# The FFN's second product, from the second group on, as seven block products in place of eight

## The chip, the cores and the metric

The kernel runs on one core of a Trainium2 chip. The metric is the device time of one execution in microseconds (us); less is better. The profile adds one execution that the hardware profiler recorded, with the time of each instruction on each engine: PE (TensorE, matmuls; PEld, its weight loads), DVE (VectorE), ACT (ScalarE), POOL (GpSimd) and SP (SyncE, which issues most DMAs).

## The reference

Attention with four sink keys and a window of 128, a Fourier mix over positions and features, a LayerNorm and an FFN:

```python
keep = is_sink | in_window                    # 4 sinks, window 128
a = softmax(where(keep, q @ k.T / sqrt(64), -1e9))
x = concat_heads(a @ v)                       # [4, 768, 512]
u = x + real(fft(fft(x, axis=1), axis=2))
un = (u - mean(u)) / sqrt(var(u) + 1e-06)
out = u + relu(un @ w_ch1) @ w_ch2            # 512 -> 2048 -> 512
```

There are 4 x 768 = 3072 rows. The weights arrive as 64-bit floats; everything else is fp32.

## The kernel before

Rows are taken in 24 blocks of 128, six to a batch. The first part of the program (up to about 222 us) computes attention and the Fourier mix and leaves u in SBUF or DRAM; its order is not touched by the change. The FFN follows, in groups of blocks (`sizes`): 4, 2, 4, 4, 4, 4, 2. The 2048 hidden features are 16 chunks f of 128.

Every fp32 operand of a product is split in a high and a low part of the matmul's input type, and a product is three matmuls (high x high, high x low, low x high). For each group and each f:

- `ch1` (L609): 4 x 3 = 12 matmuls of W1's chunk f against un, transposed, over all the group's rows at once (512 columns for four blocks, 256 for two), into one PSUM bank of two that take turns;
- `relu` (L1099, ACT) writes the high part of relu(h) to SBUF and `relu_lo` (L1104, DVE) the low part, from PSUM;
- `ch2` (L1111): for each block three matmuls with 512 columns, that block's h as weights and W2's chunk f moving, summed over f in one bank for each block.

`advance` (L1215) issues the ch2 of the step before behind the ch1 of the present one, so PE alternates between 12 matmuls of each kind. After f = 15, `finish` adds u to each bank on DVE (L1115) and stores the block (L1116, SP). During a group, `prepare` (L1138) makes the next group's un: LayerNorm's statistics (L504, L505), the inverse deviations (a chain of small steps, `deviations`), un itself (`un_make`, L528), its transposition, and the split in high (`un_hi`, L538, ACT) and low (`un_lo`, L543, DVE). In groups 1 and 2 the transposition is on PE (`un_turn`, L534), from group 3 on it is 16 small transposes for a block on DVE (L1135). It is a generator; three of its steps run for each f. Group 0's un is turned on PE too.

Group 0's FFN (222 to 335 us) also converts the weights: `convert` (L574) makes fp32 of the two words of a 64-bit value in three DVE steps (L580 to L582), the high part on ACT (L597) and the low part on POOL (L598), for W1 and W2 alike. Both parts of all the weights then stay in SBUF. Some are kept in tiles that earlier stages had used: `w_ring` (f = 0, 1), and `gh` and `gl` of the Fourier mix (`W_FOLD`). Up to the end of group 0 a scheduler orders the instructions; from group 1 on the loop at L1224 to L1241 is a manual schedule, and each engine runs in the order of the code.

Of the kernel before, what the change touches and what calls it, by code (L numbers as in the profile page):

```python
# [46 lines left out]
W_FOLD = 12  # L47
# [7 lines left out]
PREP_N = 3  # L55
PREP_AT, PREP_M = 1, 3
RELOAD_AT = 1
# [86 lines left out]
PARTS_TAIL = ((1,) * 5, 1, 1)  # L144

# [60 lines left out]
def kernel(  # L206
# [17 lines left out]
    def f32(ap):  # L224
        return ap.bitcast(F32)
# [25 lines left out]
    sizes = [4, 2, 4, 4, 4, 4, 2]  # L251
# [8 lines left out]
    def run(general):  # L260
        tag = "g" if general else ""
        with ExitStack() as p1:
# [301 lines left out]
            Wt, raw, state = {}, {}, {}  # L564
# [8 lines left out]

            def convert(i, pool=None):  # L574

                r = raw.pop(i)
                t = npool.tile([P, 512], I32, tag="qs0", name=f"cv{i}", bufs=QSB)
# [12 lines left out]
                elif W_FOLD <= i < W_FOLD + NHALF:  # L590

                    if i == W_FOLD:
                        state["fold"] = [npool.tile([P, NHALF, DM], F32R, tag=t, name=f"w_{t}", bufs=1) for t in ("gh", "gl")]
                    d = [t[:, i - W_FOLD] for t in state["fold"]]
# [4 lines left out]
                Wt[divmod(i, 2)] = d  # L599
# [13 lines left out]
            def start_ffn(s):  # L613
                state["h"] = p1.enter_context(tc.tile_pool(name="ps_h" + tag, bufs=2, space=PSUM))
# [470 lines left out]
            wa = p1.enter_context(tc.tile_pool(name="wa" + tag, bufs=1, side="right"))  # L1085
            pg = ExitStack()
            g0 = pg.enter_context(tc.tile_pool(name="g0" + tag, bufs=1, side="right"))
            def relu(g, f, ps):
                tb = P * len(groups[g])
                if g == 0 and un_last:  # L1090

                    t = un_last[0][:, 1].rearrange("p i c t -> p (i c t)")
                    h = [t[:, 1024 * (f % 2) + 512 * i:1024 * (f % 2) + 512 * i + 512] for i in range(2)]
                elif g == 0:
                    h = [g0.tile([P, tb], F32R, tag=f"h{i}", name=f"h{i}_{g}_{f}", bufs=2) for i in range(2)]
                else:
                    h = npool.tile([P, 2, tb], F32R, tag="ld", name=f"h_{g}_{f}", bufs=LDB)
                    h = [h[:, 0], h[:, 1]]
# [7 lines left out]
            def ch2(f, h, po):  # L1106
                w = Wt[f, 1]
                for i in range(len(po)):
# [29 lines left out]
            def prepare(g):  # L1138
# [12 lines left out]
                for i, u in enumerate(us):  # L1151
# [3 lines left out]
                    if g <= 2:  # L1155

                        pool, tag = banks[1 if g == 1 else i % 2][:2]
# [9 lines left out]
                    un_hi(b, blk, unT, i)  # L1167
                    un_lo(b, blk, unT, i)
# [4 lines left out]
            un_last = []  # L1173
            with (tc.manual_schedule() if MAN0 else ExitStack()):
# [10 lines left out]
                for f in range(NF):  # L1185
                    ps = hp.pop(0) if f < 2 else ch1(0, f, unT0)
                    if f == PREP:
# [3 lines left out]
                        un_last.append(wl.tile([P, 2, 2, NCC, 2 * P], F32R, name="un_last"))  # L1191
                    hs[f] = relu(0, f, ps)
# [18 lines left out]
                ch2(NF - 1, hs.pop(NF - 1), po)  # L1211
# [121 lines left out]
```

## Time and profile before

| | |
|---|---|
| median of three runs | 789.29 us (788.75 to 790.04) |
| time of the profiled execution | 788.91 us |
| its span, first to last instruction | 787.1 us |
| PE, DVE, ACT, POOL busy | 759.0, 457.9, 238.6, 177.3 us |
| granted TensorE clock, mean | 0.994 |
| group 0's FFN | about 222 to 335 us |
| groups 1 to 6 | 335 to 779 us |

A row of the timeline has start, duration, engine, line and operation, with the written tile on the left of the arrow, the read ones on its right, and then the count. In brackets stands how long the engine had been idle and on what. In the chain of waits, a row has start, duration and what ran. In a group of instructions, count and busy time stand behind the bar or the x, then the mean of one in ns, then the idle time ahead of them and who ended it. In the page's table of 40 slices each digit is a tenth of a slice:

```profile
PE   7999998999989899999999999999999999999996
DVE  6788588888899699662356514662356424511211
ACT  5777665665632223211111110111111111110110
POOL 2566377377635345300000000000000000000000
```

### The profile page before, as it was taken

The numbers are of one execution on the slowest core, as the hardware profiler recorded it, in microseconds if no ns is written. First come the engines' busy times: TensorE is split into PE (matmuls) and PEld (weight loads), VectorE is DVE, ScalarE is ACT, GpSimd is POOL, SyncE is SP. The second block draws the span as 40 slices with busy tenths as digits, with TensorE's granted clock in tenths as the row PEclk, the third lists the DMA queues.
The fourth block names the chain that finished last, engine by engine and source line by source line (L and its number), as shares of the span: only waits on it lengthen the run. The fifth ranks groups of instructions, "written<-read, shape, count | busy, mean of one in ns | idle before, by whom it ended". The sixth has DMA issues, their size and how long they took to land.

```text
span 787.1 us, 11962 instructions
## 1 busy us (share of the span) xinstructions
PE 759.0 (96%) x4379; PEld 614.3 (78%) x4379; DVE 457.9 (58%) x1354; ACT 238.6 (30%) x704; POOL 177.3 (23%) x283
## 2 busy tenths in 40 slices
PE   7999998999989899999999999999999999999996
PEld 5666776766778778899888888888888888888895
DVE  6788588888899699662356514662356424511211
ACT  5777665665632223211111110111111111110110
POOL 2566377377635345300000000000000000000000
PEclk9999999999999999999999999999999999999998
DMA  9844516433214356120100002000200001000100
GB/s 307 268 115 137 139 55 197 127 111 130 68 33 154 135 187 214 55 107 1 54 1 0 1 0 107 1 1 0 81 1 0 1 5 49 1 1 0 54 1 32
DMA packets 41811, 57.68 MB, mean 73 GB/s; under 512 B 2796, under 2 KB 27500, under 8 KB 41360
## 3 DMA queue, kind: packets, MB, share of 16 engines
q1 hardware_dynamic: 41456, 53.07, 21.2%
q0 software_dynamic: 288, 3.76, 1.2%
q8 instruction: 37, 0.61, 0.3%
q14 instruction: 30, 0.25, 0.1%
HBM read 47.37 MB, written 9.45 MB: 72 GB/s over the span
## 4 chain that ended last, share of the span: by engine, by line
PE 82%; DVE 11%; issue 2%; ACT 2%; POOL 1%; DMA 1%; SPq 0%; ACTq 0%; DVEq 0%; POOLq 0%
PE o L1111 32%; PE h L609 32%; PE xt L779 4%; PE s L692 4%; PE pt L741 2%; PE za L384 2%; DVE f L341 1%; PE zb L384 1%; DVE cv L581 1%; DVE cv L580 1%; PE x L791 1%; DVE sm L710 1%; PE zr L384 1%; DVE cv L582 1%; DVE gl L357 1%
## 5 line engine op out<-in xcount | busy, mean ns | idle before, releaser
L1111 PE MATMUL o<-w,h 128*128 128x512 f32 x876 | 216.9, 395 | 0.0
L1104 DVE SCALAR_TENSOR_TENSOR h<-h,h 128x512 fp32r<-128x512 f32 (+1 forms) x107 | 65.4, 611 | 243.8 <-ACT h L1099 243.6
L1111 PEld LDWEIGHTS o<-w,h 128*128 128x128 f32 x876 | 164.0, 189 | 34.5
L1099 ACT ACTIVATE h<-h 128x512 fp32r<-128x512 f32 (+1 forms) x107 | 57.1, 534 | 360.5 <-PE h L609 360.5
L609 PE MATMUL h<-un_slots,w 128*128 128x512 f32 (+1 forms) x576 | 123.7, 363 | 0.9 <-POOL w L598 0.9
L609 PEld LDWEIGHTS h<-un_slots,w 128*128 128x128 f32 x576 | 99.8, 188 | 19.4 <-POOL w L598 1.4
L609 PE MATMUL h<-un_last,w 128*128 128x512 f32 (+1 forms) x432 | 88.6, 354 | 0.0
L609 PEld LDWEIGHTS h<-un_last,w 128*128 128x128 f32 x432 | 72.8, 189 | 12.4
L716 ACT ACTIVATE sm<-sm,mx 128x132 f32<-128x132 f32 x192 | 75.9, 400 | 14.4 <-DVE mx L710 14.4
L1135 DVE STREAM_TRANSPOSE unf<-un 32x128 f32<-32x128 f32 x224 | 67.7, 302 | 3.2
L692 PE MATMUL s<-ring,q 64*128 64x260 f32 x320 | 55.1, 426 | 7.6 <-DVE mx L710 7.5
L710 DVE CUSTOM_DVE_ANT_0 sm<-s,mask 128x132 f32<-128x132 f32 x192 | 47.5, 284 | 3.9 <-PE s L690 2.0
L698 DVE COPY_PREDICATED s<-older,s 128x256 f32<-128x256 uint8 x80 | 33.7, 422 | 14.5 <-PE s L692 14.3
L692 PEld LDWEIGHTS s<-ring,q 64*128 64x128 f32 x320 | 24.8, 185 | 21.7 <-issue 10.3
L598 POOL TENSOR_TENSOR w<-cv,w 128x512 fp32r<-128x512 f32 x25 | 33.7, 1349 | 31.1 <-ACT w L597 31.1
L779 PE MATMUL xt<-ptl,ldv 128*64 128x128 f32 x384 | 39.0, 285 | 0.0
L716 ACT ACTIVATION_READ_ACCUMULATOR sm<-sm,mx 128x1 f32 x192 | 36.8, 192 | 0.0
L1111 PE MATMUL o<-w_ring,h 128*128 128x512 f32 x144 | 35.6, 393 | 0.0
L757 POOL TENSOR_SCALAR_AFFINE_SELECT ptl<-pta 128x512 f32<-128x512 f32 x48 | 32.4, 675 | 13.4 <-ACT pta L748 10.1
L748 ACT COPY pta<-pt 128x512 f32<-128x512 f32 x48 | 28.0, 584 | 19.1 <-PE pt L741 18.5
L779 PEld LDWEIGHTS xt<-ptl,ldv 128*64 128x64 f32 x384 | 21.8, 136 | 14.2 <-issue 6.9
L779 PE MATMUL xt<-pta,ldv 128*64 128x128 f32 x320 | 31.7, 274 | 0.1
(197 smaller groups left out, 1042.3 us busy)
## 6 DMA issues: line engine op xcount, KB each, us to landing
raw<-in_moe_w_ch_dram SPq DMA_DIRECT2D x32, 512.0 KB, 3.5
ldv<-in_v_dram SPq DMA_DIRECT2D x28, 256.0 KB, 2.7
ring<-in_qk_dram SPq DMA_DIRECT2D x24, 264.0 KB, 4.7
out_dram<-u SPq DMA_DIRECT2D x24, 256.0 KB, 3.6
q<-in_qk_dram SPq DMA_DIRECT2D x20, 256.0 KB, 4.8
cst<-in_dft_dram POOLq DMA_DIRECT2D x1, 3348.0 KB, 12.9
ud<-us SPq DMA_DIRECT2D x12, 256.0 KB, 2.1
u<-ud SPq DMA_DIRECT2D x2, 1024.0 KB, 4.9
```

The costliest lines, as they stand in the source:

```text
L598: G.tensor_tensor(d[1], tf, f32(d[0]), op=ALU.subtract)
L609: T.matmul(ps[:, :tb], a[:, cs], x[:, :, cc, :], start=n == 0, stop=n == 3 * NCC - 1)
L692: T.matmul(ps[:, j, :P + W], st["q", g][rows, hp, :], keys(g, 2 * hp + j), start=True, stop=True)
L698: V.copy_predicated(ps[:, :, P + NS:P + W], older[qi > 2], ps[:, :, 0:P])
L710: V.tensor_tensor_reduce(sm[:, h % 4], ps[:, j, P:P + W], mask[min(qi, 3)], -SCALE, 3.0e38, ALU.add, ALU.min, accum_out=mx[:, 0, h:h + 1])
L716: A.activation(sm[:, h % 4], sm[:, h % 4], AF.Exp, bias=mx[:, 0, h:h + 1], scale=-1.0, accum_out=mx[:, 1, h:h + 1])
L757: G.affine_select(lo, a, [[0, 4], [s, P]], compare_op=ALU.is_ge, fill=0.0, base=0, channel_multiplier=-s)
L779: T.matmul(ps[D * j:D * j + D, p, :], st["v", kb(g) - i][:, h, :], a[:, h % 4, :], start=i == 0, stop=i == n - 1)
L1099: A.activation(h[0], ps[:, :tb], AF.Relu)
L1104: V.scalar_tensor_tensor(h[1], ps[:, :tb], 0.0, f32(h[0]), op0=ALU.max, op1=ALU.subtract)
L1111: T.matmul(po[i], a[:, ts_], x, start=f == 0 and n == 0, stop=f == NF - 1 and n == 2)
L1135: V.transpose(unf[32 * q:32 * q + 32, :, r], un[r].rearrange("p (c q j) -> p c q j", c=NCC, q=4)[:, :, q])
```

## The change

All groups have four blocks. Group 0's second product stays as it was. From group 1 on the second product of two chunks f (2q and 2q + 1) is taken as a product of 2 x 2 blocks. The left matrix is h: two row halves (the group's first and last two blocks, A1x and A2x) by two chunks. The right one is W2: two chunks by two halves of 256 output columns. Seven products of sums of such blocks replace the eight (Strassen's scheme in Winograd's form). With S1 = A21 + A22, S2 = S1 - A11, S3 = A11 - A21, S4 = A12 - S2 and the sums T1 to T4 on W2's side, the left factors are, in order, A11, S3, A12, A22, S1, S2, S4. The seven products are summed over q in seven PSUM banks, so ch1 has one bank (`h0`) from then on. A product is two row tiles x 3 matmuls of 256 columns, 42 for a pair of chunks in place of 24 of 512.

The sums are made in fp32 and split afterwards. So relu writes fp32 (`r4`), and DVE makes S1 to S4 (L1252 to L1261), ACT the high parts (L1247) and DVE the low parts (L1248). W2 stays in fp32 (`w2r`); for each group and pair, POOL makes T1 to T4 (L1272 to L1275), ACT copies their high parts (L1283) and POOL subtracts for the low parts (L1284); in the last group DVE takes two of these. Group 0 keeps W2's split parts in three turning tiles, and POOL rebuilds W2 for f = 0 and 1 from them. The tiles of split sums are single. PE issues, for each q, ch1 of 2q, the first half of the products of q - 1 (`slot`, products 0, 1, 2 and half of 3), ch1 of 2q + 1, and the second half. At a group's end the seven sums are combined and added to u: `finish_a` (a copy on ACT and four additions on DVE), `finish_b` (one) and `finish_c` (four) run in the first two pairs of the next group, `finish_d` (three additions on POOL, then the stores) in the pairs after. `finish_last` does it for the last group. `prepare` of group 1 has four blocks, turned on PE; from group 2 on all is turned on DVE.

```diff
-W_FOLD = 12
+W_FOLD = 6
...
-PREP_N = 3
+PREP_N = 4
...
-RELOAD_AT = 1
+RELOAD_AT = 4
...
+LEFT = ("A11", "S3", "A12", "A22", "S1", "S2", "S4")
+RIGHT = (0, 0), (1, 0), (0, 1), (1, 1), (2, 0), (2, 1), (3, 0)
...
-    sizes = [4, 2, 4, 4, 4, 4, 2]
+    sizes = [4] * 6
...
+                if which and f >= 2:
+                    t = w2_raw(f, pool)
...
+                    d = state["w2t", f % 3]
...
-                ps = state["h"].tile([P, 512], F32, tag="h", name=f"h_{g}_{f}")
+                ps = state["h"].tile([P, 512], F32, tag=f"h{f % 2 if g == 0 else 0}", name=f"h_{g}_{f}")
...
+            for f in range(2):
+                G.tensor_tensor(w2_raw(f, wa).bitcast(F32), *(f32(x) for x in Wt[f, 1]), op=ALU.add)
...
-                    if g <= 2:
-
-                        pool, tag = banks[1 if g == 1 else i % 2][:2]
+                    if g == 1:
+                        pool, tag = banks[1][:2]
...
+                    if g > 1:
+                        yield
...
+                        hc.append(wl.tile([P, 2, len(LEFT) * 2 * P], F32R, name="h_sums"))
+                        hc.append(wl.tile([P, 2, 2 * P], F32R, name="w2t3"))
...
-                ch2(NF - 1, hs.pop(NF - 1), po)
-                finish(0, po, us)
...
+            sums = [npool.tile([P, 4, 2 * P], F32, tag="ld", name=f"sums{i}", bufs=LDB) for i in range(3)]
+            r4, hs4, wt4 = sums
+            r4 = r4.rearrange("p (f t) w -> p f t w", f=2)
+            hc_hi, hc_lo = hc[0][:, 0], hc[0][:, 1]
+            WC = [state["w2t", i] for i in (1, 2, 0)] + [[hc[1][:, i] for i in range(2)]]
...
+            def split_h(src, a, n):
+                A.copy(hc_hi[:, left(a, n)], src)
+                V.tensor_tensor(hc_lo[:, left(a, n)], src, f32(hc_hi[:, left(a, n)]), op=ALU.subtract)
+            def first_h():
+                V.tensor_tensor(hs4[:, 0], r4[:, 0, 0], r4[:, 0, 1], op=ALU.subtract)
+                split_h(r4[:, 0, 0], 0, 1)
+                split_h(hs4[:, 0], 1, 1)
+            def second_h():
+                V.tensor_tensor(hs4[:, 1], r4[:, 0, 1], r4[:, 1, 1], op=ALU.add)
+                split_h(r4[:, 1].rearrange("p t w -> p (t w)"), 2, 2)
+                V.tensor_tensor(hs4[:, 2], hs4[:, 1], r4[:, 0, 0], op=ALU.subtract)
+                V.tensor_tensor(hs4[:, 3], r4[:, 1, 0], hs4[:, 2], op=ALU.subtract)
+            def third_h():
+                split_h(hs4[:, 1:4].rearrange("p t w -> p (t w)"), 4, 3)
+            def w_sums(q):
+                x = Wr[q].bitcast(F32).rearrange("p f (d w) -> p f d w", d=2)
+                (b11, b12), (b21, b22) = [[x[:, i, j] for j in range(2)] for i in range(2)]
+                t3, t4, t1, t2 = (wt4[:, i] for i in range(4))
+                G.tensor_tensor(t3, b22, b12, op=ALU.subtract)
+                G.tensor_tensor(t1, b12, b11, op=ALU.subtract)
+                G.tensor_tensor(t2, b22, t1, op=ALU.subtract)
+                G.tensor_tensor(t4, b21, t2, op=ALU.subtract)
+            def split_w(q, i, eng=G):
+                x = Wr[q].bitcast(F32).rearrange("p f (d w) -> p f d w", d=2)
+                c, k, src, n = ((0, 0, x[:, :, 0], 2), (1, 0, wt4[:, 0:1], 1), (1, 1, wt4[:, 1:2], 1),
+                                (2, 0, wt4[:, 2:4], 2), (3, 0, x[:, 1:2, 1], 1))[i]
+                hi, lo = (t[:, 2 * P * k:2 * P * (k + n)].rearrange("p (n w) -> p n w", n=n) for t in WC[c])
+                A.copy(hi, src)
+                eng.tensor_tensor(lo, src, f32(hi), op=ALU.subtract)
+            def product(acc, q, i, tp):
+                a, (c, k) = i, RIGHT[i]
+                hi, lo = (t[:, 2 * P * a + P * tp:2 * P * a + P * tp + P] for t in (hc_hi, hc_lo))
+                w_hi, w_lo = (t[:, 2 * P * k:2 * P * k + 2 * P] for t in WC[c])
+                for n, (x, w) in enumerate(((hi, w_hi), (hi, w_lo), (lo, w_hi))):
+                    T.matmul(acc[i][:, 2 * P * tp:2 * P * tp + 2 * P], x, w, start=q == 0 and tp == 0 and n == 0,
+                             stop=q == NF // 2 - 1 and n == 2, skip_group_check=True)
...
+            def finish_a(g, acc):
+                (x11, _), (x21, x22) = halves(g)
+                p1, p7, p2 = (bank2(acc[i]) for i in range(3))
+                state["u2"] = s = wl.tile([P, 2, 2 * P], F32, tag="u2", name=f"u2_{g}", bufs=1)
+                A.copy(s, p1)
+                add(V, x11, p1)
+                add(V, x21, p7)
+                add(V, x22, p7)
+                add(V, x11, p2)
+            def finish_b(g, acc):
+                add(V, halves(g)[1][0], bank2(acc[3]))
+            def finish_c(g, acc):
+                (x11, x12), (x21, x22) = halves(g)
+                p5, p6, p3 = (bank2(acc[i]) for i in range(4, 7))
+                s = state["u2"]
+                add(V, x12, p5)
+                add(V, x22, p5)
+                add(V, s, p6)
+                add(V, x12, p3)
+            def finish_d(g):
+                (_, x12), (x21, x22) = halves(g)
+                for x in (x12, x21, x22):
+                    add(G, x, state["u2"])
+                    yield
+                for t in (0, 1):
+                    for b, blk in groups[g][2 * t:2 * t + 2]:
+                        nc.sync.dma_start(out[b, blk], u_of(b, blk))
+            def slot(item, part):
+                if item is None:
+                    return
+                g, acc, q = item
+                for i, tp in [(i, tp) for i in range(7) for tp in range(2)][part]:
+                    product(acc, q, i, tp)
+            def finish_last(g, acc, q):
+                (x11, x12), (x21, x22) = halves(g)
+                p1, p7, p2, p4, p5, p6, p3 = (bank2(t) for t in acc)
+                s1, s2 = wl.tile([P, 2, 2 * P], F32, tag="u2", name=f"u2_{g}", bufs=1), r4[:, 0]
+                for i in range(4):
+                    for tp in range(2):
+                        product(acc, q, i, tp)
+                A.copy(s1, p1)
+                add(G, x11, s1)
+                add(V, x21, p4)
+                add(V, x11, p2)
+                for i in (5, 4, 6):
+                    for tp in range(2):
+                        product(acc, q, i, tp)
+                add(V, s1, p6)
+                add(G, x12, s1)
+                V.tensor_tensor(s2, s1, p7, op=ALU.add)
+                add(G, x21, s2)
+                add(V, x22, p5)
+                add(V, x22, s2)
+                add(V, x12, p5)
+                add(V, x12, p3)
+                for t in (1, 0):
+                    for b, blk in groups[g][2 * t:2 * t + 2]:
+                        nc.sync.dma_start(out[b, blk], u_of(b, blk))
...
+            prev, late = None, iter(())
             with tc.manual_schedule():
+                w_sums(0)
+                for i in (0, 1, 2, 4):
+                    split_w(0, i)
                 for g in range(1, len(groups)):
+                    unT = state[g][1]
+                    steps = iter(())
+                    for q in range(NF // 2):
+                        ps = ch1(g, 2 * q, unT)
+                        A.activation(r4[:, 0].rearrange("p t w -> p (t w)"), ps, AF.Relu)
+                        if prev is None:
+                            ch2(NF - 1, hs[NF - 1], po, slice(0, 2))
+                        slot(prev, slice(0, 7))
+                        first_h()
+                        if q == 1 and g > 1:
+                            finish_c(*old)
+                            late = finish_d(old[0])
+                        if prev is not None:
+                            if prev[2] == NF // 2 - 1:
+                                finish_a(*prev[:2])
+                            w_sums(q)
+                            split_w(q, 1)
+                            split_w(q, 0)
+                        for _ in range(3):
+                            next(steps, None)
+                        ps = ch1(g, 2 * q + 1, unT)
+                        A.activation(r4[:, 1].rearrange("p t w -> p (t w)"), ps, AF.Relu)
+                        if prev is None:
+                            ch2(NF - 1, hs.pop(NF - 1), po, slice(2, 4))
+                        slot(prev, slice(7, 14))
+                        second_h()
+                        if prev is None:
+                            split_w(0, 3)
+                            finish(0, po, us)
+                        else:
+                            for i in range(2, 5):
+                                split_w(q, i, V if g == len(groups) - 1 and i < 4 else G)
+                            if prev[2] == NF // 2 - 1:
+                                finish_b(*prev[:2])
+                                old = prev[:2]
+                        if q == 0:
+                            acc = accumulators(g)
+                        else:
+                            next(late, None)
+                        if q == RELOAD_AT:
                             reload(g - 1)
+                        if q == 0:
+                            if g + 1 < len(groups):
+                                steps = prepare(g + 1)
+                        next(steps, None)
+                        third_h()
+                        for _ in range(2):
                             next(steps, None)
+                        prev = g, acc, q
                     for _ in steps:
                         pass
+                finish_last(*prev)
```

How the instructions stand on the engines, in three places. First PE at the end of group 0: `unt` is a block of un being turned, `o_0` a block's bank, `h_0` and `h_15` the banks of ch1, `un_last` group 1's un. Before:

```order
L534 MATMUL unt_1_4145<-ident,un_5_4143 128x128 x4
L609 MATMUL h_15_4152<-un_slots,w_0_4094 128x512 x2
L609 MATMUL h_15_4152<-un_slots,w_1_4095 128x512
L609 MATMUL h_15_4152<-un_slots,w_0_4094 128x512 x2
...
L1111 MATMUL o_0_3262<-w_0_4103,un_last 128x512
L1111 MATMUL o_0_3262<-w_1_4104,un_last 128x512
L1111 MATMUL o_0_3262<-w_0_4103,un_last 128x512
```

and after the change:

```order
L1130 MATMUL o_0_3265<-w2t_0_3296,h_sums 128x512
L1130 MATMUL o_0_3265<-w2t_1_3297,h_sums 128x512
L1130 MATMUL o_0_3265<-w2t_0_3296,h_sums 128x512
L537 MATMUL unt_3_4168<-ident,un_1_4166 128x128 x4
L629 MATMUL h_0_4192<-un_last,w_ring 128x512 x12
L1130 MATMUL o_0_3262<-w_ring,h_sums 128x512 x3
L1130 MATMUL o_0_3263<-w_ring,h_sums 128x512 x3
```

The last turn stood ahead of group 0's last ch1, and 36 matmuls came between it and group 1; it now stands directly ahead of group 1's first ch1, and group 0's last ch2 has moved behind that.

Second, DVE in the middle of a group, where a block of the next one is prepared (`un` is the block, `unf` its transpose). Before:

```order
L1104 SCALAR_TENSOR_TENSOR h_6_5419<-h_6_5406,h_6_5419 128x512
L1135 STREAM_TRANSPOSE unf_1_5434<-un_3_5404 32x4x32 x12
L1104 SCALAR_TENSOR_TENSOR h_7_5460<-h_7_5447,h_7_5460 128x512
L1135 STREAM_TRANSPOSE unf_1_5434<-un_3_5404 32x4x32 x4
L543 TENSOR_TENSOR un_slots<-unf_1_5434,un_slots 128x4x128
```

and after the change (`sums_4175` is r4, relu's output; `sums_4176` holds S1 to S4; `h_sums` the split parts):

```order
L1252 TENSOR_TENSOR sums_4176<-sums_4175 128x256
L1248 TENSOR_TENSOR h_sums<-sums_4175,h_sums 128x256
L1248 TENSOR_TENSOR h_sums<-sums_4176,h_sums 128x256
L1154 STREAM_TRANSPOSE unf_0_5333<-un_0_5283 32x4x32 x12
L1258 TENSOR_TENSOR sums_4176<-sums_4175 128x256
L1248 TENSOR_TENSOR h_sums<-sums_4175,h_sums 128x512
L1260 TENSOR_TENSOR sums_4176<-sums_4176,sums_4175 128x256
L1261 TENSOR_TENSOR sums_4176<-sums_4175,sums_4176 128x256
L1154 STREAM_TRANSPOSE unf_0_5333<-un_0_5283 32x4x32 x4
L1248 TENSOR_TENSOR h_sums<-sums_4176,h_sums 128x768
L546 TENSOR_TENSOR un_last<-unf_0_5333,un_last 128x4x128
```

For two chunks, two steps that read PSUM have become eight that read two operands in SBUF, around the same transposes.

Third, POOL, which had nothing to do after the last low part of a weight (`w_1<-cv`, L598) in group 0. For each pair it now has:

```order
L1272 TENSOR_TENSOR sums_4177<-w2r_3547 128x256
L1273 TENSOR_TENSOR sums_4177<-w2r_3547 128x256
L1274 TENSOR_TENSOR sums_4177<-w2r_3547,sums_4177 128x256
L1275 TENSOR_TENSOR sums_4177<-w2r_3547,sums_4177 128x256
L1284 TENSOR_TENSOR w2t_1_3297<-sums_4177,w2t_0_3296 128x256
L1284 TENSOR_TENSOR w_ring<-w2r_3547,w_ring 128x512
L1284 TENSOR_TENSOR w2t_1_3297<-sums_4177,w2t_0_3296 128x256
L1284 TENSOR_TENSOR w_ring<-sums_4177,w_ring 128x512
L1284 TENSOR_TENSOR w2t_3949<-w2r_3547,w2t_3949 128x256
```

Nine steps on POOL, 40 times, all of them added.

More of the change, by code (lines that the diff above doesn't have):

```diff
@@ L589, in convert @@
                     d = [state["ring"][:, 2 * i + j] for j in range(2)]
-                elif W_FOLD <= i < W_FOLD + NHALF:
-                    if i == W_FOLD:
+                    if which:
+                        state["w2t", f] = d
+                elif which:
+                    if f == 2:
+                        state["w2t", f] = [pool.tile([P, 512], F32R, name=f"w2t{f}_{j}") for j in range(2)]
+                    d = state["w2t", f % 3]
+                elif W_FOLD <= f < W_FOLD + NHALF:
+                    if f == W_FOLD:
                         state["fold"] = [npool.tile([P, NHALF, DM], F32R, tag=t, name=f"w_{t}", bufs=1) for t in ("gh", "gl")]
-                    d = [t[:, i - W_FOLD] for t in state["fold"]]
+                    d = [t[:, f - W_FOLD] for t in state["fold"]]
                 else:
@@ L1089, in relu @@
                 tb = P * len(groups[g])
[L1090 to L1094, printed above, removed]
+                if hc:
+                    t = hc[0].rearrange("p i t -> p (i t)")
+                    h = [t[:, 2560 * (f % 2) + 512 * i:2560 * (f % 2) + 512 * i + 512] for i in range(2)]
+                else:
                     h = [g0.tile([P, tb], F32R, tag=f"h{i}", name=f"h{i}_{g}_{f}", bufs=2) for i in range(2)]
-                else:
-                    h = npool.tile([P, 2, tb], F32R, tag="ld", name=f"h_{g}_{f}", bufs=LDB)
-                    h = [h[:, 0], h[:, 1]]
                 A.activation(h[0], ps[:, :tb], AF.Relu)
@@ L1104, in relu_lo, with ch2 @@
                 V.scalar_tensor_tensor(h[1], ps[:, :tb], 0.0, f32(h[0]), op0=ALU.max, op1=ALU.subtract)
-            def ch2(f, h, po):
+            def ch2(f, h, po, part=slice(None)):
                 w = Wt[f, 1]
-                for i in range(len(po)):
+                for i in range(len(po))[part]:
                     ts_ = slice(P * i, P * i + P)
@@ L1172, in run @@
             pw = None
-            un_last = []
+            un_last, hc = [], []
             with (tc.manual_schedule() if MAN0 else ExitStack()):
@@ new lines, in accumulators, with halves @@
+            def accumulators(g):
+                b = [banks[0][:2], banks[1][:2], (state["h"], "h1")] + [(ps_o, f"o{i}") for i in range(4)]
+                return [pool.tile([P, 512], F32, tag=t, name=f"p{i}_{g}") for i, (pool, t) in enumerate(b)]
+            def halves(g):
+                r = []
+                for t in range(2):
+                    (b, blk), (b2, blk2) = groups[g][2 * t:2 * t + 2]
+                    assert b == b2 and blk2 == blk + 1
+                    u = U[b if b in U else b - 1][:, blk:blk + 2, :]
+                    r.append([u[:, :, 2 * P * d:2 * P * d + 2 * P] for d in range(2)])
+                return r
```

42 lines of the change are left out of this document (17 added, 25 removed).

## The prediction

> **What bounds the kernel now.** I read the page's busy shares first, then the shares of the chain that ended last.
>
> ```profile
> span 787.1 us, 11962 instructions
> PE 759.0 (96%) x4379; PEld 614.3 (78%) x4379; DVE 457.9 (58%) x1354; ACT 238.6 (30%) x704; POOL 177.3 (23%) x283
> PE 82%; DVE 11%; issue 2%; ACT 2%; POOL 1%; DMA 1%; SPq 0%; ACTq 0%; DVEq 0%; POOLq 0%
> ```
>
> PE carries the chain. The other engines are averages over stages, so the next view is the table of windows: the converting of weights beside group 0 (245 to 265) against the steady FFN (380 to 470).
>
> ```profile
> 245.00:265.00 20.00, 17.82 (x83) 15.09 (x83) 18.93 (x24) 6.09 (x12) 8.74 (x7) 0.94 0.48 161
> 380.00:470.00 90.00, 90.00 (x395) 73.85 (x394) 41.73 (x113) 12.18 (x21) 0.00 (x0) 1.00 0.04 12
> ```
>
> The columns are length, PE, PEld, DVE, ACT, POOL, clock. In the first stretch PE waits 2.2 us and DVE is full; in the second PE never waits at clock 1.00, DVE is at 46%, ACT at 14% and POOL does nothing. So after group 0 the time is PE's matmuls, and three engines have room that the change fills. The chain of waits gives the matmuls' true spacing (the records of single matmuls overlap).
>
> ```profile
> 326.92 0.44 PE unt L534 x4
> 330.13 5.44 PE o L1111 x24
> 366.99 1.43 PE h L609 x12
> 368.42 1.37 PE o L1111 x6
> 387.90 2.75 PE o L1111 x12
> 390.65 2.72 PE h L609 x12
> 393.37 2.81 PE o L1111 x12
> 776.57 2.79 PE o L1111 x12
> 779.35 0.02 issue
> ```
>
> Twelve matmuls with 512 columns take 2.72 us (0.227 each), 2.81 at worst; twelve with 256 columns 1.43 us (0.119 each), each with weights of its own, as the products will have them. A block turned on PE costs 0.44. From the end of the 24 matmuls at 330.13 + 5.44 = 335.57 to 779.35, groups 1 to 6 hold 443.8 us.
>
> **The change, part by part.** *PE after group 0.* A group of four now has 16 first products (13 at 2.72, three from the fold's tiles at up to 2.81: 43.8) and 8 pairs of f with 42 matmuls of 256 columns (336 x 0.119 = 40.0). That is 83.8 a group and 419.2 for five, in place of 443.8: **-24.6 us**. In it, a pair's second product falls from 24 x 0.227 = 5.44 to 42 x 0.119 = 5.01, the 256-column first products of the two groups of two are gone, and so are four blocks' turns on PE (4 x 0.44). Only a seventh of the arithmetic of one of two products is saved, and little more than half of that arrives as time: 48 x 0.119 would be 5.72, above the 5.44 paid now. A period of one pair is 2 x 2.72 + 5.01 = 10.45 us; the others must fit in it.
>
> *What a pair costs DVE.* Durations from the groups of instructions, by form:
>
> ```profile
> L1135 DVE STREAM_TRANSPOSE unf<-un 32x128 f32<-32x128 f32 x224 | 67.7, 302 | 3.2
> L504 DVE BATCH_NORM_STATS2 bn<-u 128x6 f32<-128x512 f32 x24 | 16.1, 675 | 0.3 <-POOL u L449 0.3
> L505 DVE BATCH_NORM_AGGREGATE stat<-bn 128x2 f32<-128x6 f32 x24 | 4.3, 181 | 0.7
> L1115 DVE TENSOR_TENSOR u<-o,u 128x512 f32<-128x512 f32 x24 | 15.5, 685 | 3.3 <-PE o L1111 3.3
> L528 DVE TENSOR_SCALAR un<-u,stat 128x512 f32<-128x512 f32 x24 | 13.1, 544 | 0.2
> L543 DVE TENSOR_TENSOR un_last<-unf,un_last 128x512 fp32r<-128x512 f32 x8 | 5.5, 692 | 5.5 <-ACT un_last L538 5.5
> L598 POOL TENSOR_TENSOR w<-cv,w 128x512 fp32r<-128x512 f32 x25 | 33.7, 1349 | 31.1 <-ACT w L597 31.1
> L597 ACT CAST w<-cv 128x512 fp32r<-128x512 f32 x25 | 15.5, 622 | 35.0 <-DVE cv L582 35.0
> L1099 ACT ACTIVATE h<-h 128x512 fp32r<-128x512 f32 x75 | 44.8, 598 | 284.0 <-PE h L609 284.0
> L1099 ACT ACTIVATE h<-h 128x256 fp32r<-128x256 f32 x32 | 12.3, 384 | 76.5 <-PE h L609 76.5
> L580 DVE TENSOR_SCALAR cv<-raw 128x512 int32<-128x512 int32 x14 | 10.7, 764 | 1.2 <-POOL w L598 1.2
> L1111 PEld LDWEIGHTS o<-w,h 128*128 128x128 f32 x876 | 164.0, 189 | 34.5
> ```
>
> And four rows of the timeline where DVE and POOL add in 256-wide pieces side by side, then two where a 512-wide one meets a 512-wide one (start, duration):
>
> ```profile
> 225.54 0.41 DVE L437 TENSOR_TENSOR d<-asb,b 128x257 f32<-128x257 f32 x1
> 225.87 0.41 DVE L438 TENSOR_TENSOR d<-asb,b 128x257 f32<-128x257 f32 x1
> 226.21 0.83 DVE L448 TENSOR_TENSOR u<-u,d 128x257 f32<-128x257 f32 x1
> 226.96 0.85 DVE L449 TENSOR_TENSOR u<-u,d 128x255 f32<-128x255 f32 x1
> ...
> 226.03 0.73 POOL L449 TENSOR_TENSOR u<-u,d 128x255 f32<-128x255 f32 x1 [2.22 <-DVE d L437]
> 226.71 0.82 POOL L448 TENSOR_TENSOR u<-u,d 128x257 f32<-128x257 f32 x1
> ...
> 245.88 1.72 DVE L581 SCALAR_TENSOR_TENSOR cv<-raw,cv 128x512 int32<-128x512 int32 x1
> ...
> 245.75 1.29 POOL L598 TENSOR_TENSOR w<-cv,w 128x512 fp32r<-128x512 f32 x1 [1.28 <-ACT w L597]
> ```
>
> Alone a 256-wide addition on DVE comes every 0.33 us (225.54 to 225.87). A pair's eight (six of 256, one of 512 at 0.692 - 0.08 = 0.61, one of 768, estimated at 0.61 + 0.28) take 3.5 us. In the first pair of a group five additions from PSUM (3.4) and three blocks' statistics (3 x 0.856) come on top: 9.5; the second pair is about the same; the pairs in which a block is prepared carry 0.54 + 16 x 0.302 + 0.69 = 6.1 more: 9.6. Six such pairs are about 57 us of 62.7, so there is room for **0.9 us of waiting in a pair**.
>
> *The waiting.* Side by side, DVE's addition stretched from 0.41 to 0.83 and ended 0.28 after POOL's had (226.76 to 227.04); POOL's next ended 0.49 after DVE's (227.53). At 245.88 DVE ended 0.56 after POOL. So they take turns, holding 0.28 and 0.56 (DVE, 256 and 512) and 0.49 (POOL, 256); POOL at 512 then holds about 1.29 - 0.14 = 1.15. A pair has on POOL seven pieces of 256 and two of 512, on DVE six, one and one: 7 x 0.49 + 2 x 1.15 + 6 x 0.28 + 0.56 + 0.84 = 8.8 us of 10.45 (9.4 where a block is prepared). The turns fit, but each of DVE's eight can wait up to 1.15. POOL's work for a pair comes mostly right after PE frees the tiles, DVE's right after the relus, so I take three or four waits of 0.4, 1.2 to 1.6 a pair, against room of 0.9. The bounds are 0 and, if all eight wait a mean 0.3, 2.4.
>
> The Trainium skill, page "SBUF — State Buffer", section "Who interferes with whom", calls the shared port pair of VectorE and GpSimd an exclusive lock under which the second instruction waits until the first ends. By that rule a pair would take 11.2 us on the port (worked out under the rivals), by the pitches above 8.8; the rows show the turns, and an overlap of about 0.14 at each.
>
> *What DVE's delay costs.* The second relu of a pair is ready at 2.72 + 2.5 + 2.72 + 0.6 = 8.5 us, the copy behind it at 9.2 and DVE's four steps on it at about 10.7. The next pair's first relu overwrites what these read; it must end before PE, behind half a slot, refills the one bank of ch1, at 10.45 + 5.23 - 0.6 = 15.1. So a delay of up to **4.4 us** in a group is free. With 1.5 of waiting the six pairs run 3.6 behind: just free; with 2.4, 9 behind, and PE waits 4.6 in each of four groups. Besides, ACT (two relus 1.2, copies of h and W at 0.38 for 256 and 0.62 for 512, about 4.6: 5.8 us of 10.45) has relus queued behind copies that wait for DVE or POOL, and at the group's third or fourth pair the casts of un come in between. I take 1.5 us for each of groups 1 to 4 and 1 for the last, which has no preparing: **+7 us**, with ends 0 and 25.
>
> *Group 0 and its end.* Two more blocks turned on PE: +0.9. DVE, which is full from 225 to 265, gets two blocks' statistics (1.7 us), POOL two additions of 512 for the raw W2 (2 x 1.29), in turn with DVE; against that, W2's conversions no longer wait for a buffer that POOL's subtraction reads (the row of L580 onto cv shows 1.2 us of such idle time). I take **+1.3**, with ends -1.2 and +4.3. Then the last block's turn stands directly ahead of group 1's first product, which must wait for un's high half on ACT (0.59) and low half on DVE (0.69), perhaps behind two casts (1.24): **+1.5**, with ends 1.3 and 2.6. Before, two whole products lay between.
>
> *The end.* Before, one addition follows the last matmul, then the stores:
>
> ```profile
> 778.68 1.39 DVE L1115 TENSOR_TENSOR u<-o,u 128x512 f32<-128x512 f32 x2 [1.24 <-PE o L1111]
> 779.40 1.02 SPq L1116 DMA_DIRECT2D out_dram<-u  x2
> ```
>
> Now the sums run on. The product of s1 ends 1.43 before the last matmul; s1, s2 and x22 + p5 take DVE to 0.64 after it, x22 + s2 takes its turn behind POOL's two (1.29 each, to 1.84) and ends at 2.4, two more of 0.69 at 3.8. The last addition of before ended at 0.72: **+3.1**, with ends 1.5 and 4.
>
> *Sum.* 787.1 - 24.6 + 0.9 + 1.3 + 1.5 + 7 + 3.1 = 776.3 us of span. The profiled run took 788.91, 1.8 more than its span, and lies 0.4 below the median of the three; so 778.1 us, on the profiled run's own scale.
>
> **The rivals.** *All covers hold.* The waits stay under the free 4.4 us: without the 7 and with the low ends of the rest, 765 to 771. For it: 57 of 62.7 us and 8.8 of 10.45. Against: ACT and the port have queues that no row of before shows full.
>
> *DVE and POOL set the pace (slower).* If whole durations exclude each other, POOL's seven pieces at half of 1.29 and two at 1.29 (7.1) and DVE's six at 0.41, one at 0.69 and one at about 0.95 (4.1) make 11.2 us a pair in place of 10.45, 11.9 with un's low half in it: 40 pairs x 0.75 = 30, and 16 x 0.69 = 11 more in the pairs that prepare. That makes 776.3 - 7 + 41 + 1.8 = 812. With half of that excess, or waits of 2.4 a pair and stalls of 18 to 25, it is 790 to 796. It turns to slower where stalls pass 18 us (0.45 us a pair). The rows bear out the taking of turns, not the whole duration. The Trainium skill's rule named above would work in this way. Also no row shows a transpose beside POOL (idle after 335); if transposes take turns too, 16 x 0.302 joins the 9.4 and the period is over 14 us in 16 pairs: past 830.
>
> *The 256-column products are slower than 0.119.* The weights' loads last 0.189 alone by the page's group of L1111; two halves of one bank alternate. At 5.44 / 42 = 0.130 the gain on the second product is gone: 1680 x 0.011 = 18 us, 796. Against: the 1.43 row has new weights at each matmul too.
>
> *The seven products are not what runs.* The order on PE shows 42 in a pair, so I give this nothing.
>
> **How the numbers follow.** Forecast (771 to 784) 0.46; covers hold (765 to 771) 0.19; between 784 and 790 0.08; DVE and POOL set the pace (790 up) 0.20, of it 0.05 above 802; slow matmuls (about 796) 0.07. The range of 767 to 802 leaves out about 0.15. A measurement tells about 0.2% (1.6 us) from no change: faster 0.68, same 0.06, slower 0.26.
>
> **What would show it.** After: the chain of waits with x6 pieces of L1292 at 0.71 to 0.72 and L609's successor at 2.72 right or wrong on the main term; PE's busy time in a window of a middle group near 100% (covers hold) or near 93% with relus or h_sums as releasers (port); two-operand additions of DVE at 0.41 or stretched to 0.8 beside POOL; DVE's busy share near 95% in the first six pairs; a gap of 1.5 us ahead of group 1's first product; 10.9 us from the last matmul to the span's end. The forecast is wrong if PE's spacing is not 0.119, if transposes stretch beside POOL, or if the waiting in a pair is far from 1.5.

## The result: 850.0 us, slower by 7.6%

The changed kernel took 850.01 us (median of 4 runs, 845.63 to 851.95) against 789.33 us before: a ratio of 1.076 (95% interval 1.072 to 1.080). The forecast was 778.1, the range ended at 802. The profiled execution took 850.29 us. The profile after, the page's busy times, the granted TensorE clock in 40 slices and the shares of the chain that ended last:

```profile
span 848.5 us, 14292 instructions
PE 766.2 (90%) x4899; PEld 641.7 (76%) x4899; DVE 714.5 (84%) x1636; ACT 409.2 (48%) x1053; POOL 543.2 (64%) x644
PEclk9999999999989999989999989989999998999998
PE 59%; DVE 28%; issue 6%; ACT 4%; POOL 2%; DMA 1%; SPq 0%; ACTq 0%; DVEq 0%; POOLq 0%
```

The chain has moved from PE (82% before) to PE and DVE. The windows from the first relu of a group to that of the next show where: group 2, then most of group 5, up to its eighth pair (columns as before: length, PE, PEld, DVE, ACT, POOL, clock).

```profile
437.40:542.30 104.90, 91.84 (x530) 80.89 (x530) 93.95 (x167) 46.42 (x94) 75.97 (x76) 0.93 0.06 21
...
750.70:824.20 73.50, 73.50 (x462) 66.50 (x462) 58.26 (x81) 40.32 (x81) 53.58 (x53) 1.00 0.04 15
```

Group 5, in which nothing is prepared, runs at PE's pace: PE is busy in all of the 73.5 us, and from the second pair on (760.04) to the eighth (823.26) a pair takes 10.5 us, the period forecast as 10.45. Group 2 takes 104.9 us where eight such pairs would take 84. DVE alone is busy for 94, and PE both stands idle (13.1 us) and runs at a granted clock of 0.93. Groups 1 to 4 took 99.6, 104.9, 103.5 and 104.9 us, by the starts of the first relus.

One stall in the chain of waits, in group 3 (start, duration, what ran):

```profile
595.41 0.96 DVE h_sums L1248
596.37 0.03 issue
596.40 0.30 DVE unf L1154
...
597.70 0.02 ACT un_slots L541
597.72 0.50 issue
598.22 0.60 ACT sums L1396
598.82 0.04 issue
598.87 4.61 PE h L629 x12
603.48 2.51 PE p L1292 x21
```

and PE's timeline there:

```profile
593.38 0.52 PE L1292 MATMUL p<-w2t,h_sums 128*128 128x256 f32 x3
598.87 0.68 PE L629 MATMUL h<-un_last,w 128*128 128x512 f32 x1 [4.96 <-ACT sums L1396]
```

PE waits 4.96 us for the relu that frees ch1's single bank. That relu (L1396) stands on ACT behind un's high part (L541), which waits for DVE's sixteenth transpose, and DVE is late. Then PE's first twelve matmuls take 4.61 us in place of 2.72, at a granted clock of 0.52 (598.87 to 602.40): the idle time is paid again in clock, by four tenths. In other gaps the relu stands behind a copy of h's sums (L1247) that waits for DVE's L1261. From group 1's first product (334.96) to the last (837.12) PE is idle for 51.4 us: 37.0 behind relus, 8.8 behind h's low parts (L1248) and 5.2 behind the additions that empty the seven banks (L1314). No gap of PE, and no wait of ACT, is ended by POOL. Ten groups of twelve matmuls run slow; with a few products beside them that is about 21 us more.

DVE's groups of instructions by form show why it is late:

```profile
L1154 DVE STREAM_TRANSPOSE unf<-un 32x128 f32<-32x128 f32 x256 | 77.5, 303 | 4.2
L1248 DVE TENSOR_TENSOR h_sums<-sums,h_sums 128x256 fp32r<-128x256 f32 x80 | 47.0, 602 | 4.1 <-ACT h_sums L1247 3.7
...
L1260 DVE TENSOR_TENSOR sums<-sums,sums 128x256 f32<-128x256 f32 x40 | 37.3, 932 | 0.0
...
L1314 DVE TENSOR_TENSOR u<-u,p 128x512 f32<-128x512 f32 x42 | 26.4, 677 | 0.1
L531 DVE TENSOR_SCALAR un<-u,stat 128x512 f32<-128x512 f32 x24 | 19.0, 792 | 2.7 <-PE unt L537 2.5
```

The additions of 256 take 0.60 and 0.93 us in place of 0.41, and making un (L531) 0.79 in place of 0.54. Transposes (0.303, before 0.302) and additions from PSUM (0.677, before 0.685) are not stretched. The timeline shows the turns, POOL's rows first:

```profile
423.63 0.94 POOL L1284 TENSOR_TENSOR w2t<-sums,w2t 128x256 fp32r<-128x256 f32 x1 [1.59 <-ACT w2t L1283]
424.53 1.47 POOL L1284 TENSOR_TENSOR w_ring<-sums,w_ring 128x512 fp32r<-128x512 f32 x1
...
423.89 0.96 DVE L1260 TENSOR_TENSOR sums<-sums,sums 128x256 f32<-128x256 f32 x1
424.88 1.40 DVE L1261 TENSOR_TENSOR sums<-sums,sums 128x256 f32<-128x256 f32 x1
...
353.16 1.30 POOL L1284 TENSOR_TENSOR w_ring<-w2r,w_ring 128x512 fp32r<-128x512 f32 x1
...
355.13 1.29 POOL L1284 TENSOR_TENSOR w_ring<-sums,w_ring 128x512 fp32r<-128x512 f32 x1
...
353.39 1.10 DVE L514 TENSOR_SCALAR stat<-stat 128x4 f32<-128x4 f32 x1
354.52 0.68 DVE L516 TENSOR_SCALAR stat<-stat 128x4 int32<-128x4 int32 x1
355.23 1.21 DVE L519 SCALAR_TENSOR_TENSOR stat<-stat 128x4 f32<-128x4 f32 x1
```

Both additions end 0.28 us after the POOL step beside them (424.57 and 426.00). The last three rows are steps of the inverse deviations: four elements a partition, 0.17 us before, now 0.7 to 1.2 each, in a chain of fourteen. In this chain seven of the fourteen are stretched, in the one of group 2 five.

### The profile page after: what moved, and what is told of

The parts are those of the page before. It is cut to its first block, busy times and chain, and to the rows that moved or that the text cites. A ratio compares the mean times of both kernels' runs of the same rounds, so it can differ in the third digit from the quotient of the medians.

```text
span 848.5 us, 14292 instructions
## 1 busy us (share of the span) xinstructions
PE 766.2 (90%) x4899; PEld 641.7 (76%) x4899; DVE 714.5 (84%) x1636; ACT 409.2 (48%) x1053; POOL 543.2 (64%) x644
## 4 chain that ended last, share of the span: by engine, by line
PE 59%; DVE 28%; issue 6%; ACT 4%; POOL 2%; DMA 1%; SPq 0%; ACTq 0%; DVEq 0%; POOLq 0%
PE h L629 23%; PE p L1292 12%; DVE unf L1154 6%; PE o L1130 5%; DVE h_sums L1248 5%; PE xt L799 4%; PE s L712 4%; PE za L387 2%; PE pt L761 2%; DVE sums L1260 2%; DVE u L1314 1%; PE zb L387 1%; DVE sums L1258 1%; DVE f L344 1%; DVE un L531 1%
## 5 line engine op out<-in xcount | busy, mean ns | idle before, releaser
L1247 ACT CAST h_sums<-sums 128x256 fp32r<-128x256 f32 (+2 forms) x160 | 90.7, 567 | 185.1 <-DVE sums L1261 113.0
L1248 DVE TENSOR_TENSOR h_sums<-sums,h_sums 128x256 fp32r<-128x256 f32 (+2 forms) x160 | 137.8, 869 | 15.3 <-ACT h_sums L1247 9.9
L1292 PE MATMUL p<-w_ring,h_sums 128*128 128x256 f32 x960 | 136.3, 284 | 14.0 <-DVE h_sums L1248 8.8
L1292 PEld LDWEIGHTS p<-w_ring,h_sums 128*128 128x128 f32 x960 | 126.6, 191 | 18.7 <-DVE h_sums L1248 9.9
L1284 POOL TENSOR_TENSOR w2t<-sums,w2t 128x256 fp32r<-128x256 f32 x72 | 59.6, 828 | 112.2 <-ACT w2t L1283 111.8
L629 PE MATMUL h<-un_slots,w 128*128 128x512 f32 x396 | 108.6, 428 | 16.4 <-ACT sums L1396 16.2
L629 PE MATMUL h<-un_last,w 128*128 128x512 f32 x396 | 104.2, 415 | 18.1 <-ACT sums L1396 14.7
L1292 PE MATMUL p<-w2t,h_sums 128*128 128x256 f32 x720 | 112.5, 283 | 0.0
L1292 PEld LDWEIGHTS p<-w2t,h_sums 128*128 128x128 f32 x720 | 101.0, 192 | 3.5
L1284 POOL TENSOR_TENSOR w_ring<-sums,w_ring 128x512 fp32r<-128x512 f32 x32 | 46.0, 1437 | 12.4 <-ACT w_ring L1283 11.7
L1284 POOL TENSOR_TENSOR w_ring<-w2r,w_ring 128x512 fp32r<-128x512 f32 x40 | 53.2, 1330 | 0.5 <-ACT w_ring L1283 0.5
L1258 DVE TENSOR_TENSOR sums<-sums 128x256 f32<-128x256 f32 x40 | 30.6, 766 | 26.7 <-ACT sums L1413 26.4
L747 POOL CAST sk<-sm 128x32 fp32r<-128x32 f32 x48 | 11.7, 244 | 64.6 <-ACT sm L736 64.6
L1284 POOL TENSOR_TENSOR w2t<-w2r,w2t 128x256 fp32r<-128x256 f32 x40 | 37.5, 938 | 20.0 <-ACT w2t L1283 20.0
```

Of the source, the lines that this page charges most:

```text
L629: T.matmul(ps[:, :tb], a[:, cs], x[:, :, cc, :], start=n == 0, stop=n == 3 * NCC - 1)
L1247: A.copy(hc_hi[:, left(a, n)], src)
L1248: V.tensor_tensor(hc_lo[:, left(a, n)], src, f32(hc_hi[:, left(a, n)]), op=ALU.subtract)
L1258: V.tensor_tensor(hs4[:, 1], r4[:, 0, 1], r4[:, 1, 1], op=ALU.add)
L1284: eng.tensor_tensor(lo, src, f32(hi), op=ALU.subtract)
L1292: T.matmul(acc[i][:, 2 * P * tp:2 * P * tp + 2 * P], x, w, start=q == 0 and tp == 0 and n == 0, stop=q == NF // 2 - 1 and n == 2, skip_gro ...
```

## Experiments

The theory was that DVE waits for POOL's turns at SBUF, and that this waiting, on top of DVE's own work, passes PE's time. The rivals: DVE's own work is too long; the order on ACT makes the stalls; PE's matmuls are slower. That PE or ACT waits for what POOL makes is excluded by the waits above, none of which POOL ends. Four runs first; every run up to the one with four of POOL's steps left out was timed once.

**POOL's steps left out.**

```diff
-                            w_sums(q)
...
-                eng.tensor_tensor(lo, src, f32(hi), op=ALU.subtract)
+                if eng is V or q == 0 and w_first:
+                    eng.tensor_tensor(lo, src, f32(hi), op=ALU.subtract)
```

> POOL's nine steps on W are left out after the first pair of group 1 (T1 to T4 and the low parts of W keep their first values); ACT's copies, DVE's steps and PE's matmuls stay. If DVE's turns behind POOL (28.7 us of stretched DVE instructions in each of groups 2 to 4) are the cause, those instructions fall back to their own durations, groups 1 to 4 take 84 to 90 us in place of 99.6 to 104.9, and the time is 775 to 795. If instead the order on ACT (a relu queued behind un's high part, which waits for DVE's transposes) is the cause by itself, the gaps at the third and fifth pair stay and the time is 815 to 835. If DVE's own work is too long, it stays above 830.

It took 779.78 us. Its page's busy times, group 2's window in it, and DVE's forms:

```profile
PE 744.7 (96%) x4899; PEld 628.3 (81%) x4899; DVE 600.2 (77%) x1636; ACT 412.3 (53%) x1053; POOL 210.4 (27%) x309
```

```profile
422.80:508.30 85.50, 84.92 (x530) 76.46 (x530) 68.54 (x167) 47.23 (x94) 3.80 (x3) 1.00 0.08 25
```

```profile
L1248 DVE TENSOR_TENSOR h_sums<-sums,h_sums 128x256 fp32r<-128x256 f32 x80 | 33.9, 424 | 8.4 <-ACT h_sums L1247 7.5
...
L1260 DVE TENSOR_TENSOR sums<-sums,sums 128x256 f32<-128x256 f32 x40 | 16.7, 418 | 0.0
L531 DVE TENSOR_SCALAR un<-u,stat 128x512 f32<-128x512 f32 x24 | 13.3, 554 | 2.8 <-PE unt L537 2.6
```

The same 167 DVE instructions take 68.5 us in place of 94.0: 25.4 us of waiting in a group, 3.2 in a pair. PE's clock is back at 1.00 and the group at 85.5 us. Between 337.0 and 765.7 us PE is idle for 2.0 us in place of 51.4, and its busy time on the page is 21.5 us shorter for the same 4899 matmuls: together about the 70 us between the two runs. ACT's order and all of DVE's own work are still there, so neither makes the loss by itself.

**un's high part behind the relu.**

```diff
-                    un_hi(b, blk, unT, i)
+                    if g > 1:
+                        turned.append((b, blk, unT, i))
+                        continue
...
                         A.activation(r4[:, 0].rearrange("p t w -> p (t w)"), ps, AF.Relu)
+                        for x in turned:
+                            un_hi(*x)
```

> un's high part is issued on ACT behind the next pair's first relu, in place of ahead of it, and its low part on DVE behind that relu's three steps; nothing else changes. If the order on ACT is a cause of its own, the pairs of 15.4 and 14.3 us in groups 2 to 4 fall to 11 to 12.5 and the time to 815 to 830. If DVE is simply behind through its turns with POOL, the wait moves to another place and the time stays within 840 to 850.

The edit also drops one pause of `prepare` for each block. 837.24 us: below the 840 of "the wait only moves", short of the 830 of "a cause of its own". The fourth and sixth pair of group 2 went from 15.4 and 14.3 to 14.7 and 12.3 us, the fifth from 11.5 up to 14.6. DVE's time hardly changed:

```profile
434.50:535.30 100.80, 89.82 (x530) 78.98 (x530) 93.67 (x167) 45.69 (x94) 76.68 (x76) 0.97 0.07 22
```

So the order on ACT made a late DVE cost some 13 us more, and most of the wait moved elsewhere.

**W's split sums loaded.** Group 1 stores each pair's split sums, groups 2 to 5 load them.

```diff
-                            w_sums(q)
-                            split_w(q, 1)
-                            split_w(q, 0)
+                            if g == 1:
+                                w_sums(q)
+                                split_w(q, 1)
+                                split_w(q, 0)
+                                move_w(q, 0, False)
+                            else:
+                                move_w(q, 0, True)
```

> Group 1 makes W's split sums as before and stores them to DRAM (1.8 MB for a pair); groups 2 to 5 load them by DMA in place of making them on POOL and ACT. If DVE's turns behind POOL are the cause, groups 2 to 5 take 84 to 88 us each and group 1 keeps its 99.6: 785 to 800. If only ACT's order is the cause, groups 2 to 4 keep some 10 us of stalls each: 810 to 825. If the loads (175 GB/s) can't keep up, PE waits for them and the time is above 850.

798.13 us, with all outputs computed. Groups 1 and 2:

```profile
337.00:437.00 100.00, 89.46 (x504) 78.44 (x503) 85.58 (x161) 43.91 (x89) 62.50 (x64) 0.93 0.39 152
437.00:523.80 86.80, 84.81 (x526) 75.81 (x525) 69.39 (x168) 30.30 (x55) 3.80 (x3) 1.00 0.62 199
```

POOL working: clock 0.93 and 100 us. The next eight pairs with POOL all but idle: 1.00 and 86.8. The time lies in the 785 to 800 expected if DVE's turns behind POOL are the cause.

**Both edits.** The last two diffs together.

> The two edits before together: W's split sums loaded by DMA in groups 2 to 5, and un's high part behind the relu. If turns with POOL and ACT's order add up to the whole loss, groups 2 to 5 are bound by PE at 84 to 85 us each and only group 1 still loses: 780 to 792. If ACT's order adds nothing once DVE is on time, it equals the run with the loads alone within 3 us.

796.70 us, 1.4 from the run with the loads alone, within the 3 expected: ACT's order adds nothing once DVE is on time. It is above the 780 to 792 expected of the sum, since group 1 still took 97 us.

**A busy POOL that reads nothing.**

```diff
+                else:
+                    G.memset(idle[:, :600 * n if n == 1 else 1024], 0.0)
...
+                            for _ in range(4):
+                                G.memset(idle[:, :600], 0.0)
```

> As the run without POOL's steps, but POOL fills a spare tile nine times in each pair instead (600 or 1024 elements a partition, about 0.6 and 1.0 us by the 0.413 us of the memsets of 384 in the trace): POOL is as busy as in the change but reads nothing from SBUF. W's sums and low parts are left out. If DVE waits for what POOL reads, DVE's instructions keep their own durations and the time is 775 to 790. If it waits whenever POOL runs an instruction that touches SBUF, DVE's steps stretch as in the change and the time is above 825.

777.10 us. POOL was busy for 53.6 of group 2's 85.4 us (in the change 76.0 of 104.9), DVE for 68.8, nearly as without POOL's steps (68.5). Group 2's window, two of the three rows of POOL's fills, then rows of DVE between 345 and 765 us (here L1262 is the step that was L1260):

```profile
421.00:506.40 85.40, 84.75 (x530) 76.35 (x529) 68.84 (x167) 47.09 (x93) 53.60 (x75) 1.00 0.08 26
```

```profile
L1413 POOL MEMSET idle<- 128x600 f32 x156 | 95.4, 611 | 8.2
L1289 POOL MEMSET idle<- 128x1024 f32 x70 | 67.4, 963 | 4.0
```

```profile
L1262 DVE TENSOR_TENSOR sums<-sums,sums 128x256 f32<-128x256 f32 x39 | 16.3, 418 | 0.0
L531 DVE TENSOR_SCALAR un<-u,stat 128x512 f32<-128x512 f32 x16 | 10.4, 647 | 0.1
L514 DVE TENSOR_SCALAR stat<-stat 128x4 f32<-128x4 f32 x4 | 3.2, 794 | 0.1
L519 DVE SCALAR_TENSOR_TENSOR stat<-stat 128x4 f32<-128x4 f32 x16 | 2.7, 166 | 0.4
```

What stops a two-operand step on DVE is POOL's reading, not its being busy: 25 of the 39 L1262 and all 16 L519 ran beside a fill and kept their own times. Steps with one operand and scalars (L531, L514) still wait for fills.

**Four of POOL's nine steps left out.**

```diff
-                            w_sums(q)
                             split_w(q, 1)
```

> The change with only T1 to T4 left out in the loop (four of POOL's nine steps of a pair; they keep the values of the first pair), the five subtractions of the low parts stay. If each POOL step makes DVE wait about the same, DVE's waiting in a group falls from 28.7 to about 16 us and the loss of 70 us against the run without POOL's steps by nearly half: 810 to 820. If the loss only begins where DVE's own 69.5 us and its waiting pass the 84 us of PE, hardly more than the run without POOL's steps: 782 to 795.

822.27 us, a little above the 810 to 820 of "each step makes DVE wait about the same". The page of this run:

```profile
PE 755.0 (92%) x4899; PEld 633.2 (77%) x4899; DVE 657.6 (80%) x1636; ACT 410.4 (50%) x1053; POOL 400.1 (49%) x488
```

DVE's busy time lies midway between 714.5 with all steps and 600.2 without: half of the waiting, and 42.5 of the 70.2 us of loss. There is no threshold that hides the first half. Nor does DVE's sum over a group decide, as the second expectation had it: in group 2 of this run DVE was busy for 83.1 us, less than the 84 that PE needs, and the group took 97.7.

```profile
431.70:529.41 97.71, 88.73 (x530) 78.66 (x529) 83.08 (x168) 46.77 (x93) 45.93 (x43) 0.97 0.07 22
```

**A version of it.** Two groups with eight products; while group 1 runs, W's split sums are made once and stored, and groups 2 to 5 load them.

```diff
+                for f in range(NF):
+                    ps = ch1(0, f, unT)
+                    h = relu(1, f, ps)
+                    relu_lo(1, ps, h)
...
+                    ch2(lf, lh, lpo)
...
+                    if f % 2:
+                        w_sums(f // 2)
+                        split_t(f // 2)
```

> Groups 0 and 1 with eight products; during group 1 POOL and ACT make W's split sums once and store them to DRAM, and groups 2 to 5 load them, with seven products. DVE's work in group 1 reads PSUM for the low part of relu, so few of its steps wait for POOL. finish_d's additions come in the last three pairs, away from the statistics. If turns with POOL were the whole loss: group 1 takes 88 to 90 us, groups 2 to 4 84 to 86 each, and the time is 775 to 784, below both kernels. If group 1's DVE steps still wait long, group 1 takes 95 to 100 and the time is 785 to 792. If the small DMAs (1 KB rows) can't keep up, PE waits for W and it is above 800.

781.81 us (4 runs, 780.02 to 783.22) against 790.60 for the kernel before on the same chip: ratio 0.988 (0.984 to 0.991). Two small waits stood out. finish_d's three additions, put in the last three pairs in the code, ran in the second:

```profile
527.12 3.80 POOL L1347 TENSOR_TENSOR u<-u,u 128x512 f32<-128x512 f32 x3 [100.42 <-DVE u L1347]
...
528.47 1.22 DVE L516 TENSOR_SCALAR stat<-stat 128x4 int32<-128x4 int32 x1
529.73 1.22 DVE L519 SCALAR_TENSOR_TENSOR stat<-stat 128x4 f32<-128x4 f32 x1
```

An otherwise empty engine runs a step as soon as its inputs are there, wherever the code puts it. And the first loads of group 2 stood on SP behind a store that waited for POOL's last step. With these and two more mends (in the text on record below, "group 1's second pair" is a slip for that of groups 3 and 4, which took 12.5 and 13.9 us):

```diff
-                    add(G, x, state["u2"])
+                    add(V, x, state["u2"])
...
-                    if f % 2:
+                    if f == NF - 1:
+                        for c in (1, 0, 2, 3):
+                            load_w2(0, c)
+                    if f % 2 == 0:
                         w_sums(f // 2)
                         split_t(f // 2)
```

> The run with two classical groups and loaded split sums, with four mends: group 0's last ch2 ahead of group 1's first ch1, group 1's W work on POOL one chunk earlier and the loads of group 2's first pair ahead of the last stores, and finish_d's three additions on DVE, in the last three pairs (POOL ran them early, beside the statistics: the second pair took 12.5 us). Group 1's second pair back to 10.5 us where it was 12.5 to 13.9 (5 us in all), 3 us at the start of group 2 and 1.4 at the start of group 1: 771 to 776. If the additions on DVE cost what they saved, 776 to 780.

778.15 us (4 runs, 777.22 to 779.42) against 790.32 (7 runs, 787.30 to 792.74): ratio 0.985 (0.981 to 0.988). That is 2 us above what was expected for all four mends, in the 776 to 780 of additions on DVE that cost what they saved; group 3's fourth pair took 12.2 us, group 4's second 11.7. Groups 1 to 3 in its windows:

```profile
337.00:428.00 91.00, 89.26 (x387) 71.96 (x386) 51.51 (x114) 27.70 (x51) 64.12 (x63) 1.00 0.50 183
428.00:509.90 81.90, 81.90 (x500) 73.50 (x499) 62.99 (x162) 29.72 (x52) 0.00 (x0) 1.00 0.59 193
509.90:594.30 84.40, 84.40 (x532) 76.39 (x531) 68.15 (x170) 30.46 (x54) 0.00 (x0) 1.00 0.58 188
```

## Why the prediction was wrong, step by step

*PE after group 0, -24.6 us: right.* Products have x21 in 2.51 us and pairs in 10.5. With POOL's reading away the time fell to 777 to 780. The sum without its term for stalls is 771; a period of 10.52 in place of 10.45 (2.8 us in 40 pairs), about 1 us of stalls in a group and a tail of 12.3 us make up most of the rest.

*What a pair costs DVE: about right as a sum.* In the run without POOL's steps the eight pairs of group 2 took DVE 68.5 us; the forecast was 57 for six and little more than 3.5 for each of the others, 64.

*The waiting, 1.2 to 1.6 us a pair with 2.4 as the bound: this is the step that failed.* It measured 3.2 us a pair, above the bound. The turns were read rightly (0.28 us behind POOL's end, as forecast), and the last group, in which nothing is prepared, shows that they do fit in its period. The number of waits was about right and their length was not: in group 2, 35 of the 64 additions were stretched, 4.4 a pair, by a mean of 0.63 us in place of 0.4 (or of 0.3 in the bound). That alone is 2.8 us a pair, since POOL's steps run back to back and DVE's four on the second relu (L1258 to L1261) meet them most (18 of the 22 us). The prediction took only these eight to wait; the making of un and its low part (2.8 us in the group) and the steps of four elements (3.6 us, each stretched one by 0.5 to 1.0) wait as well. Counted step by step that makes 28 us in the group; the difference of the two runs is 25.4, since finish_d on POOL still makes DVE wait in the run without the nine steps.

*What DVE's delay costs: the room of 0.9 us a pair and the free 4.4 us were right in kind, the +7 wrong in size.* With 3.2 in place of 1.5, DVE's own 68.5 and its waiting of 25.4 make 94 us in a group of 84; the 4.4 us are gone by the second pair. The room is also not the same in each pair. Three pairs take PE 31.6 us; between the first relus of group 2's second and fifth pairs DVE was busy for 31.8 us without POOL's steps, 38.8 with five of them and 42.9 with all nine (windows 433.36 to 467.75, 442.22 to 483.65 and 448.36 to 493.88 of the three runs). There the 0.9 us, a mean over six pairs, does not exist, which fits the loss with only half of the waiting; no run moved DVE's work out of these pairs to test it. Most of the stalls, 37 of 51.4 us, came where the prediction put them, at ch1's one bank, behind the relu; it also named un's casts on ACT. In place of 7 they cost 51.4.

*Missed altogether: the clock.* No term stood for matmuls that run slower after a gap; they cost about 21 us in ten places. The Trainium skill, page "TensorE: Matmul & The Clock Gate", section "Part 1: The HAM clock gate (the "warmup" mystery)", states that PE's clock falls to half after an idle window of about 3.4 us and recovers after a busy one. The long gaps agree: 4.96 us idle, then 1.9 us lost at a granted clock of 0.52, and none in the run with no such gaps. But a shorter gap could do it here:

```profile
520.31 4.61 PE L629 MATMUL h<-un_slots,w 128*128 128x512 f32 x12 [1.94 <-ACT sums L1396]
```

The matmuls behind 2.02 us of idle time at 415.41 ran at a clock of 1.00, so the length of a gap alone does not tell.

*Group 0, its end and the tail: about right.* Group 1's first product began at 334.96, with 2.7 us of ch2 moved behind it: 1.6 us earlier than forecast (the first relu of group 1 varied from 336.6 to 340.6 us among the runs that share this start). From PE's last matmul (837.12) to the span's end are 11.4 us, forecast 10.9.

*The rivals.* The slower one was the right side and half the mechanism. It had DVE and POOL exclude each other for their whole durations and set the pace in every pair. The run with five of POOL's steps excludes that: by the rival's own count they need 4.5 + 4.1 = 8.6 us of a pair (9.3 where un's low part is in it), less than PE's 10.45, and the groups still took 92.7 to 97.7 us. The last group does not test it, since DVE makes two of POOL's low parts there and the count is 10.4. What decided was not the port's sum but DVE's lateness: its own work plus its waits in the pairs where it had least room. The turning point given, 0.45 us of stalls a pair, was passed four times over. The Trainium skill's page "SBUF — State Buffer", section "Who interferes with whom", also states that tensor_scalar steps can enter two-port modes that contend, and that a POOL instruction which only writes does not hold up a step with two inputs; the fills show both. Its rule on two inputs, read onto the statistics, would have added twelve waiting steps in a group, the one on tensor_scalar six; of the fourteen statistics steps five were stretched in group 2.

## What to carry to other kernels

Before work is moved to an idle engine, ask what the busy engines then wait for: here POOL's 76 busy us in a group cost DVE 25. Count every instruction that can wait, short ones too, since its wait goes by the other engine's step and not by its own length, and set the sum against the room in the fullest stretch, not against a mean. Where operands are made again for each group, making them once and loading them can be cheaper: some 190 GB/s of DMA ran beside PE at a clock of 1.00.

## What was not expected of the hardware

A step on 128x4 elements took 1.2 us beside a 512-wide subtraction on POOL, seven times its own 0.17. Fills on POOL of 600 elements left DVE's two-operand steps at 0.418 us, and stretched a one-operand step of four elements to 0.794. PE idle for 4.96 us cost 6.9, and 1.94 us of idle time was once enough for twelve slow matmuls.
